# Block diagonal of local queries: placed by DMA, or copied there by GpSimd

## The chip, the cores and the metric

One core of one Trainium2 chip. The metric is the device time of one execution in microseconds, as the median over runs. The profile is of one further execution, with its own time.

## What is computed

```python
def _attn_ref(q, k, v):              # 8 batches, 8 heads, 576 positions, 64 wide
    scores = q @ k.T / sqrt(64)
    mask_local   = (rel >= 0) & (rel < 32)            # rel = row - column; heads 0 to 3
    mask_strided = (rel >= 0) & (same position modulo 32)   # heads 4 to 7
    attn = softmax(where(mask, scores, -1e9))
    return attn @ v

def _moe_ref(x, w_gate, w1, w2):     # x: 4608 tokens x 512; 8 experts, 1024 wide
    expert = argmax(x @ w_gate)                        # one expert a token
    gate = softmax(x @ w_gate)[expert]
    out = gate * (relu(x @ w1[expert]) @ w2[expert])
```

The attention's output, heads side by side, is the `x` of the second part. All is fp32.

## The kernel before, in words

The program has an attention stage (to about 220 us) and an expert stage. They overlap: the first experts' windows, over the tokens of the first four batches, are laid between the last batches' attention (`fillers`).

**Attention.** A batch is cut into five tasks (`BANK_PAIRS`), 40 in all. A task fills one PSUM bank of 128x512 scores. Tasks k=0 and k=1 are local, each for two heads: the 512 queries are 16 blocks of 32, and a block sees 64 keys. `wide` (L408 to L412) makes one matmul a block for both heads: the stationary operand is a block diagonal of 128x64, with head 0's 32 queries on partitions 0 to 63 and head 1's on partitions 64 to 127, and zeros elsewhere. Zeros are written once. Queries come from the host with the block as the last index, so that a block's 64 columns stand 16 floats apart:

```python
q = qkl[k][:, 0:2 * LQ].rearrange("p (q j) -> p q j", j=LB)     # L409, LB = 16
nc.tensor.matmul(sb[...], q[:, :, j], qkl[k][:, k0:k0 + 64], ...)   # L411
```

Tasks k=2 to 4 are strided heads and rests (`local` L419, `strided` L424). In every task a bf16 matmul first puts the mask into the bank (L403).

A task runs through three stages. `stage_s` makes the scores, then `softmax` (L349 to L363): maximum and subtraction on VectorE, exponential on ScalarE, sum and reciprocal on VectorE, product with the reciprocal on GpSimd (L362). `stage_t` (L453), three tasks later, transposes the probabilities on TensorE, and ScalarE moves them to SBUF. Four tasks later, values are multiplied (`av_local` L478, `av_strided` L467). A finished pair of batches is routed (`logits`, `route`), and `xrows` (L515 to L523) transposes tokens into rows: GpSimd writes the gate into 16 columns behind the row (L517), ScalarE copies the row (L521, shown as its helper's line L162), and ScalarE's queue sends it to memory (`xd`). Five row buffers rotate.

**Loads.** SP's queue issues queries and keys five tasks ahead (`load_qk`), values (`load_v`) and expert weights (`wload` L214, 1 MB each; `wsplit` L219 splits them into two parts on ScalarE, L222, and VectorE, L223). A local task takes three loads (L381 to L383): partitions 64 to 127 whole, and partitions 0 to 63 in two pieces, as head 0's queries lie in other columns than head 1's. Two buffers, `qkl`, serve k=0 and k=1.

**Order.** TensorE's order in the attention stage is the one that the program is written in. The other engines' queues are ordered by a scheduler, which plans with its own idea of durations; an engine then works strictly in that order. `issue_after` puts an instruction behind another on the same queue.

## Time and profile before

| | |
|---|---|
| median of three timed runs | 665.07 us (664.34 to 665.81) |
| profiled execution, its own time | 671.04 us |
| its span, first to last instruction | 668.8 us |
| TensorE matmul busy | 626.7 us, 94% |
| VectorE busy | 400.9 us, 60% |
| ScalarE busy | 327.3 us, 49% |
| GpSimd busy | 148.1 us, 22% |
| DMA moved | 149.85 MB, mean 224 GB/s |

In the rows, PE is TensorE's matmuls and PEld its weight loads, DVE is VectorE, ACT ScalarE, POOL GpSimd, and SP the engine whose queue issues loads. L12 is a line of the kernel. `out<-in` names what an instruction writes and reads. A matmul in fp32 shows as two records. `[1.60 <-X]` is idle time of the engine ahead of an instruction, and what ended it. Durations of matmuls that follow each other overlap; from start to start is what one costs. The granted clock is a share of TensorE's full 2.4 GHz.

### The profile page before, as it was taken

The numbers are of one execution on the slowest core, as the hardware profiler recorded it, in microseconds if no ns is written. First come the engines' busy times: TensorE is split into PE (matmuls) and PEld (weight loads), VectorE is DVE, ScalarE is ACT, GpSimd is POOL, SyncE is SP. The second block draws the span as 40 slices with busy tenths as digits, with TensorE's granted clock in tenths as the row PEclk, the third lists the DMA queues.
The fourth block names the chain that finished last, engine by engine and source line by source line (L and its number), as shares of the span: only waits on it lengthen the run. The fifth ranks groups of instructions, "written<-read, shape, count | busy, mean of one in ns | idle before, by whom it ended". The sixth has DMA issues, their size and how long they took to land.

```text
span 668.8 us, 14979 instructions
## 1 busy us (share of the span) xinstructions
PE 626.7 (94%) x6136; PEld 522.0 (78%) x6154; DVE 400.9 (60%) x788; ACT 327.3 (49%) x584; POOL 148.1 (22%) x168
## 2 busy tenths in 40 slices
PE   4999889789979999999899899999999999999996
PEld 3877778577858778888588788887898788887885
DVE  5667968656757369899424576823596235863332
ACT  1556665565645565356332555622565224753232
POOL 3232223420041021216100413200612004301021
PEclk9899999989989999899999999999999999999999
DMA  9968998994652865558933576872896546863301
GB/s 283 243 231 270 299 302 256 333 342 162 222 212 96 300 225 167 179 193 280 384 142 117 204 292 209 282 252 92 314 356 219 170 181 225 328 238 150 126 20 64
DMA packets 36550, 149.85 MB, mean 224 GB/s; under 512 B 5114, under 2 KB 5504, under 8 KB 26240
## 3 DMA queue, kind: packets, MB, share of 16 engines
q1 hardware_dynamic: 22848, 105.92, 47.1%
q10 hardware_dynamic: 7344, 22.70, 9.5%
q0 software_dynamic: 6288, 20.26, 8.3%
q8 instruction: 49, 0.80, 0.5%
q14 instruction: 21, 0.17, 0.1%
HBM read 129.69 MB, written 19.63 MB: 223 GB/s over the span
## 4 chain that ended last, share of the span: by engine, by line
PE 35%; issue 34%; POOL 7%; DMA 5%; DVE 4%; ACT 2%; POOLq 1%; ACTq 0%; another core or an unknown queue 0%
POOL xg L239 4%; PE t L297 4%; PE t L299 4%; PE t L298 4%; PE y L286 4%; PE y L287 3%; PE y L288 3%; POOL out_dram L258 2%; PE s L411 2%; DMA raw<-in_wcat_dram 1%; PE v L520 1%; DMA out_dram<-y,oids 1%; PE v L467 1%; DMA xg<-xd,eids 1%; DMA xd<-xr 1%
## 5 line engine op out<-in xcount | busy, mean ns | idle before, releaser
L223 DVE TENSOR_TENSOR wlo<-raw,whi 128x1024 fp32r<-128x1024 f32 x136 | 164.0, 1222 | 76.2 <-ACT whi L222 68.1
L222 ACT CAST whi<-raw 128x1024 fp32r<-128x1024 f32 x136 | 139.3, 1051 | 63.4 <-PE s L288 25.4
L297 PE MATMUL t<-xh,whi 128*128 128x256 f32 (+1 forms) x384 | 126.9, 332 | 2.3 <-ACT xh L231 2.1
L298 PE MATMUL t<-xl,whi 128*128 128x256 f32 (+1 forms) x384 | 124.3, 324 | 0.0
L299 PE MATMUL t<-xh,wlo 128*128 128x256 f32 (+1 forms) x384 | 123.6, 322 | 0.5 <-DVE wlo L223 0.5
L303 DVE SCALAR_TENSOR_TENSOR hl<-t,hh 128x256 fp32r<-128x256 f32 (+1 forms) x96 | 49.0, 510 | 103.2 <-ACT hh L302 102.9
L302 ACT ACTIVATE hh<-t 128x256 fp32r<-128x256 f32 (+1 forms) x96 | 43.8, 456 | 120.7 <-PE t L299 109.2
L297 PEld LDWEIGHTS t<-xh,whi 128*128 128x128 f32 x384 | 73.1, 191 | 13.3 <-ACT xh L231 3.3
L286 PE MATMUL y<-whi,hh 128*128 128x512 f32 x192 | 77.2, 402 | 2.1 <-ACT hh L302 2.1
L299 PEld LDWEIGHTS t<-xh,wlo 128*128 128x128 f32 x384 | 73.6, 192 | 6.3 <-DVE wlo L223 1.1
L298 PEld LDWEIGHTS t<-xl,whi 128*128 128x128 f32 x384 | 73.4, 191 | 5.9 <-DVE xl L232 0.3
L287 PE MATMUL y<-wlo,hh 128*128 128x512 f32 x192 | 75.9, 395 | 0.0
L288 PE MATMUL y<-whi,hl 128*128 128x512 f32 x192 | 74.6, 395 | 0.0
L362 POOL TENSOR_TENSOR prob<-prob,ri 128x512 f32<-128x512 f32 x40 | 42.5, 1063 | 122.9 <-DVE ri L361 87.6
L258 POOL DMA_INDIRECT out_dram<-y,oids x24 | 27.5, 1147 | 115.7 <-DVE y L257 110.9
L162 ACT COPY xT<-v 128x270 f32<-128x270 f32 (+1 forms) x80 | 30.1, 480 | 28.8 <-PE v L467 12.3
L286 PEld LDWEIGHTS y<-whi,hh 128*128 128x128 f32 x192 | 36.4, 189 | 9.4 <-ACT hh L302 2.9
L288 PEld LDWEIGHTS y<-whi,hl 128*128 128x128 f32 x192 | 35.9, 189 | 9.1 <-DVE hl L303 1.3
L287 PEld LDWEIGHTS y<-wlo,hh 128*128 128x128 f32 x192 | 36.5, 190 | 5.0
L358 DVE TENSOR_REDUCE sm<-prob 128x8 f32<-128x512 f32 x40 | 27.3, 683 | 21.5 <-ACT prob L356 21.2
L352 DVE TENSOR_REDUCE nm<-s 128x8 f32<-128x512 f32 x40 | 27.3, 683 | 18.5 <-PE s L411 14.0
L239 POOL DMA_INDIRECT xg<-xd,ids x24 | 30.2, 1259 | 31.9 <-ACT xh L231 18.9
(219 smaller groups left out, 1056.7 us busy)
## 6 DMA issues: line engine op xcount, KB each, us to landing
raw<-in_wcat_dram SPq DMA_DIRECT2D x68, 1024.0 KB
sraw<-in_wcat_dram ACTq DMA_DIRECT2D x12, 1024.0 KB
xd<-xr ACTq DMA_DIRECT2D x36, 264.0 KB
vl<-in_vv_dram SPq DMA_DIRECT2D x16, 512.0 KB
qkl<-in_qk_dram SPq DMA_DIRECT2D x16, 264.0 KB
vt<-in_vv_dram SPq DMA_DIRECT2D x16, 256.0 KB
qk<-in_qk_dram SPq DMA_DIRECT2D x8, 484.0 KB
qk<-in_qk_dram SPq DMA_DIRECT2D x8, 432.0 KB
```

Source lines behind the costliest of these rows:

```text
L222: nc.scalar.copy(out=hi[:, sl], in_=raw[:, sl])
L223: i = nc.vector.tensor_tensor(out=lo[:, sl], in0=raw[:, sl], in1=hi[:, sl].bitcast(F32), op=ALU.subtract)
L239: lastp[0] = nc.gpsimd.indirect_dma_start(out=xg, out_offset=None, in_=xd[0:rows, :], in_offset=bass.IndirectOffsetOnAxis(ap=idc, axis=0))
L286: nc.tensor.matmul(yb[t], hh[:, ts], whi[:, w], start=(j == 0), stop=False)
L287: nc.tensor.matmul(yb[t], hh[:, ts], wlo[:, w], start=False, stop=False)
L288: nc.tensor.matmul(yb[t], hl[:, ts], whi[:, w], start=False, stop=(j == 7))
L297: nc.tensor.matmul(hb[:, 0:n], whi[:, w], xh[:, dc, :], start=(dc == 0), stop=False)
L298: nc.tensor.matmul(hb[:, 0:n], whi[:, w], xl[:, dc, :], start=False, stop=False)
L299: nc.tensor.matmul(hb[:, 0:n], wlo[:, w], xh[:, dc, :], start=False, stop=(dc == 3))
L302: nc.scalar.activation(out=hh[:, 0:n], in_=hb[:, 0:n], func=AF.Relu)
L303: nc.vector.scalar_tensor_tensor(out=hl[:, 0:n], in0=hb[:, 0:n], scalar=0.0, in1=hh[:, 0:n].bitcast(F32), op0=ALU.max, op1=ALU.subtract)
L362: lastp[0] = nc.gpsimd.tensor_tensor(out=pv, in0=pv, in1=ri.unsqueeze(2).broadcast_to([128, 8, 64]), op=ALU.mult)
```

## The change

Queries and keys of a local task come in one load of all 128 partitions, queries in their natural order. A new tile `qbd` holds the block diagonal, block by block, 64 columns each; its zeros are written once. A new function, `spread`, copies the two heads' queries there on GpSimd, two tasks ahead of the task that reads them, and `issue_after` puts the copies behind the product of the task that was just begun. `wide` takes its weights from `qbd`, 64 floats side by side.

```diff
+AHEAD = 2
-        qkl = [loc.tile([128, 2 * LQ + LK], F32, name=f"qkl{k}") for k in range(2)]
+        qkl = [loc.tile([128, LQ + LK], F32, name=f"qkl{k}") for k in range(2)]
+        qbd = [loc.tile([128, LB, 2 * QB], F32, name=f"qbd{k}") for k in range(2)]
         for k in range(2):
-            nc.vector.memset(qkl[k][64:128, 0:LQ], 0.0)
-            nc.gpsimd.memset(qkl[k][0:64, LQ:2 * LQ], 0.0)
+            nc.vector.memset(qbd[k].rearrange("p j q -> p (j q)"), 0.0)
...
                 if k < 2:
-                    o = QKO[k]
-                    nc.sync.dma_start(out=qkl[k][64:128, LQ:], in_=qk[b, 64:128, o:o + LQ + LK])
-                    nc.sync.dma_start(out=qkl[k][0:64, 0:LQ], in_=qk[b, 0:64, o:o + LQ])
-                    nc.sync.dma_start(out=qkl[k][0:64, 2 * LQ:], in_=qk[b, 0:64, o + LQ:o + LQ + LK])
+                    nc.sync.dma_start(out=qkl[k], in_=qk[b, :, QKO[k]:QKO[k + 1]])
...
+        def spread(i):
+            if i < len(tasks) and tasks[i][1] < 2:
+                k = tasks[i][1]
+                for h in range(2):
+                    hs = slice(64 * h, 64 * h + 64)
+                    c = nc.gpsimd.tensor_copy(out=qbd[k][hs, :, QB * h:QB * h + QB],
+                                              in_=qkl[k][hs, 0:LQ].rearrange("p (j q) -> p j q", q=QB))
+                    if lastp[0] is not None:
+                        issue_after(c, lastp[0])
...
             def wide(j, i, col, last):
-                q = qkl[k][:, 0:2 * LQ].rearrange("p (q j) -> p q j", j=LB)
-                k0 = 2 * LQ + QB * j
-                nc.tensor.matmul(sb[64 * i:64 * i + 64, col:col + 64], q[:, :, j], qkl[k][:, k0:k0 + 64],
+                k0 = LQ + QB * j
+                nc.tensor.matmul(sb[64 * i:64 * i + 64, col:col + 64], qbd[k][:, j, :], qkl[k][:, k0:k0 + 64],
...
         def xrows(g, c, xT):
             xr = xrp.tile([128, XW], F32, name="xr")
-            nc.gpsimd.tensor_copy(out=xr[:, DM:XW], in_=gates[g][:, c:c + 1].broadcast_to([128, XW - DM]))
...
             evac(X_ENG[c % 2], xr[:, 0:DM], xb)
+            nc.scalar.copy(out=xr[:, DM:XW], in_=gates[g][:, c:c + 1].broadcast_to([128, XW - DM]))
...
         load_qk(0)
+        spread(0)
...
         load_qk(1)
+        spread(1)
...
                     pvs[i] = stage_s(*tasks[i])
+                    spread(i + AHEAD)
                     load_qk(i + NBK)
```

Smaller edits: the masks of three kinds of task become overlapping stretches of one tile, with 1,152 columns cast at the start instead of 1,536; the input tiles of tasks 2 to 4 get a buffer each of their exact width, where three equal buffers rotated; a table of 32 columns in `slot_tables` is made in a scratch buffer; the host no longer reorders the queries.

The scheduler also orders the queues anew. On GpSimd's queue, from the first softmax product on, gates stood between products (`xr` is a row buffer, `gt` the gates). Before:

```order
L362 TENSOR_TENSOR prob<-prob,ri 128x512 x9
L517 COPY xr<-gt 128x16 x3
L362 TENSOR_TENSOR prob<-prob,ri 128x512 x5
L517 COPY xr<-gt 128x16 x3
L362 TENSOR_TENSOR prob<-prob,ri 128x512
L517 COPY xr<-gt 128x16 x2
```

Now:

```order
L391 COPY qbd_137<-qkl_135 64x16x32 x2
L391 COPY qbd_138<-qkl_136 64x16x32 x2
L362 ISA
L362 TENSOR_TENSOR prob<-prob,ri 128x512 x4
L391 COPY qbd_137<-qkl_135 64x16x32 x2
L362 TENSOR_TENSOR prob<-prob,ri 128x512
L391 COPY qbd_138<-qkl_136 64x16x32 x2
L362 TENSOR_TENSOR prob<-prob,ri 128x512 x4
```

The gates are gone, and the copies for a local task stand right behind the product of the task two before it.

On SP's queue, at the turn from the second batch's loads to the third's (`vl` and `vt` are values, `raw` expert weights). Before:

```order
L387 DMA qk<-in_qk_dram 128x864
L394 DMA vt<-in_vv_dram 128x512
L381 DMA qkl_135<-in_qk_dram 64x1056
L382 DMA qkl_135<-in_qk_dram 64x512
L383 DMA qkl_135<-in_qk_dram 64x544
L394 DMA vl<-in_vv_dram 128x1024
L381 DMA qkl_136<-in_qk_dram 64x1056
```

Now:

```order
L401 DMA vt_360<-in_vv_dram 128x512
L384 DMA qk_358<-in_qk_dram 128x864
L215 DMA raw<-in_wcat_dram 128x2048
L380 DMA qkl_135<-in_qk_dram 128x1056
L401 DMA vl<-in_vv_dram 128x1024 x2
L380 DMA qkl_136<-in_qk_dram 128x1056
```

A first load of expert weights has moved ahead of the third batch's queries, and three more follow in the next 21 rows; before, the first stood some forty rows further on.

The splits of these weights on ScalarE and VectorE move with their loads: the first `whi` (L222, now L223) now stands between the two copies of the first batch's local values.

On VectorE's queue, at the first softmax (`nm` maximum, `sm` sum, `ri` reciprocal). Before:

```order
L352 TENSOR_REDUCE nm<-s 128x8
L355 TENSOR_TENSOR prob<-s,nm 128x512
L352 TENSOR_REDUCE nm<-s 128x8
L358 TENSOR_REDUCE sm<-prob 128x8
L355 TENSOR_TENSOR prob<-s,nm 128x512
L360 TENSOR_SCALAR ri<-sm 128x8
```

Now:

```order
L352 TENSOR_REDUCE nm<-s 128x8
L355 TENSOR_TENSOR prob<-s,nm 128x512
L352 TENSOR_REDUCE nm<-s 128x8
L355 TENSOR_TENSOR prob<-s,nm 128x512
L352 TENSOR_REDUCE nm<-s 128x8
L358 TENSOR_REDUCE sm<-prob 128x8 x2
L360 TENSOR_SCALAR ri<-sm 128x8
```

The first sum stood behind the second task's maximum; it now stands behind the third's.

## Rows read from the trace of the kernel before

**Rows 1.** Windows: length, busy us (instructions) PE, PEld, DVE, ACT, POOL; clock, DMA share, GB/s
```profile
42.00:61.50 19.50, 18.96 (x389) 14.20 (x389) 12.91 (x33) 11.23 (x26) 5.31 (x6) 1.00 0.83 259
61.50:83.00 21.50, 19.85 (x417) 16.70 (x419) 18.99 (x56) 14.09 (x30) 6.14 (x11) 1.00 0.87 275
...
104.00:125.00 21.00, 19.03 (x415) 16.09 (x414) 18.42 (x61) 13.92 (x30) 7.35 (x12) 1.00 0.90 283
125.00:145.00 20.00, 15.68 (x246) 13.18 (x252) 9.65 (x25) 9.30 (x19) 7.03 (x10) 0.91 0.99 318
...
300.00:668.00 368.00, 357.39 (x2243) 299.52 (x2241) 190.31 (x248) 165.49 (x265) 73.01 (x62) 0.99 0.59 211
```

**Rows 2.** Instructions of lines L411 and L478: duration ns min/median/max, first and last start
```profile
L411 PEld LDWEIGHTS s<-qkl x512: 184/206/228, 6.8 to 181.9; 128*64 128x64 f32 x171
...
L478 PEld LDWEIGHTS v<-pTl,vl x512: 132/138/158, 24.3 to 217.0; 128*64 128x64 f32 x171
```

**Rows 3.** Timeline of PE: start us, us, engine, line, operation
```profile
43.89 2.03 PE L478 MATMUL v<-pTl,vl 128*64 128x64 f32 x64
45.86 0.66 PE L520 MATMUL y<-cst,xT 128*128 128x128 f32 x4
...
47.09 2.06 PE L411 MATMUL s<-qkl 128*64 128x64 f32 x32
49.09 0.66 PE L453 MATMUL t<-cst,prob 128*128 128x128 f32 x4
```

**Rows 4.** Timeline of the start, all engines
```profile
6.85 2.12 PE L411 MATMUL s<-qkl 128*64 128x64 f32 x32 [1.60 <-DMA qkl<-in_qk_dram]
...
12.24 0.81 PE L424 MATMUL s<-qk 64*54 64x54 f32 x24
...
14.49 1.04 POOL L362 TENSOR_TENSOR prob<-prob,ri 128x512 f32<-128x512 f32 x1 [8.93 <-DVE ri L361]
...
15.58 1.12 PE L453 MATMUL t<-cst,prob 128*128 128x128 f32 x4 [2.54 <-POOL prob L362]
```

**Rows 5.** Windows of 2 us, columns as in rows 1
```profile
4.00:6.00 2.00, 0.58 (x1) 0.10 (x1) 1.36 (x6) 0.00 (x0) 1.25 (x2) 1.00 1.11 250
10.00:12.00 2.00, 2.00 (x37) 1.66 (x39) 0.75 (x2) 0.64 (x1) 0.00 (x0) 1.00 1.01 393
16.00:18.00 2.00, 2.00 (x27) 1.38 (x27) 0.12 (x1) 1.24 (x3) 1.04 (x1) 0.50 1.06 227
```

**Rows 6.** Instructions of single lines on POOL and DVE, columns as in rows 2
```profile
L371 POOL MEMSET qkl<- x2: 515/516/518, 0.8 to 1.2; 64x512 f32 x2
...
L362 POOL TENSOR_TENSOR prob<-prob,ri x40: 1037/1043/1823, 14.5 to 214.2; 128x512 f32<-128x512 f32 x40
...
L517 POOL COPY xr<-gt x36: 187/196/1184, 41.6 to 246.3; 128x16 f32<-128x16 f32 x36
...
L370 DVE MEMSET qkl<- x2: 485/485/485, 1.2 to 1.8; 64x512 f32 x2
```

**Rows 7.** Page, part 5: group xcount | busy us, mean ns of one | idle before, releaser
```profile
L358 DVE TENSOR_REDUCE sm<-prob 128x8 f32<-128x512 f32 x40 | 27.3, 683 | 21.5 <-ACT prob L356 21.2
L352 DVE TENSOR_REDUCE nm<-s 128x8 f32<-128x512 f32 x40 | 27.3, 683 | 18.5 <-PE s L411 14.0
```

**Rows 8.** Waits of POOL to 300 us: us in total, times, longest us
```profile
POOL prob L362 <- DVE ri L361: 87.6, 26, 9.7
...
POOL xr L517 <- DMA xd<-xr: 22.3, 3, 13.6
```

**Rows 9.** Timeline of SP's issues and of POOL: a load and a product
```profile
46.86 0.47 SPq L381 DMA_DIRECT2D qkl<-in_qk_dram  x1
...
58.49 1.04 POOL L362 TENSOR_TENSOR prob<-prob,ri 128x512 f32<-128x512 f32 x1 [1.48 <-DVE ri L361]
```

**Rows 10.** Chain of waits: start us, us, what (a DMA from issue to landing)
```profile
83.19 9.06 DMA raw<-in_wcat_dram
```

**Rows 11.** Timeline of ACT, a small copy
```profile
192.92 0.20 ACT L162 COPY xT<-v 128x64 f32<-128x64 f32 x1
```

More of the change, by code (lines that the diff above doesn't have):

```diff
@@ L183, in moe_attn @@
     wg_sb = const.tile([128, 4, 32], F32, name="wg_sb")
-    mask_b = const.tile([128, 3, 8, 64], BF16, name="mask_b")
+    mask_b = const.tile([128, 18, 64], BF16, name="mask_b")
     tri_b = const.tile([128, 128], BF16, name="tri_b")
@@ L320, in moe_attn @@
     with ExitStack() as actx:
-        inp = actx.enter_context(tc.tile_pool(name="inp", bufs=NBK - 2))
+        inp = actx.enter_context(tc.tile_pool(name="inp", bufs=1))
         loc = actx.enter_context(tc.tile_pool(name="loc", bufs=1))
@@ L334, in make_masks @@
         def make_masks():
-            for k, kinds in enumerate((((0, 1, 1), (1, 8, 0)), ((0, 2, 0), (2, 8, 2)), ((0, 8, 2),))):
-                for x0, x1, m in kinds:
-                    nc.vector.tensor_copy(out=mask_b[:, k, x0:x1, :],
-                                          in_=lmask_f[:, 64 * m:64 * m + 64].unsqueeze(1).broadcast_to([128, x1 - x0, 64]))
+            for x0, x1, m in ((0, 1, 1), (1, 10, 0), (10, 18, 2)):
+                nc.vector.tensor_copy(out=mask_b[:, x0:x1, :],
+                                      in_=lmask_f[:, 64 * m:64 * m + 64].unsqueeze(1).broadcast_to([128, x1 - x0, 64]))
         def load_more():
@@ L379, in load_qk @@
                 if k < 2:
-                    o = QKO[k]
-                    nc.sync.dma_start(out=qkl[k][64:128, LQ:], in_=qk[b, 64:128, o:o + LQ + LK])
-                    nc.sync.dma_start(out=qkl[k][0:64, 0:LQ], in_=qk[b, 0:64, o:o + LQ])
-                    nc.sync.dma_start(out=qkl[k][0:64, 2 * LQ:], in_=qk[b, 0:64, o + LQ:o + LQ + LK])
+                    nc.sync.dma_start(out=qkl[k], in_=qk[b, :, QKO[k]:QKO[k + 1]])
                     return
-                t = inp.tile([128, max(QKW[2:])], F32, name="qk")
+                t = inp.tile([128, QKW[k]], F32, name=f"qk{k}")
                 loaded[b, "qk", k] = t
                 nc.sync.dma_start(out=t[:, 0:QKW[k]], in_=qk[b, :, QKO[k]:QKO[k + 1]])
+        def spread(i):
[7 more added lines that the diff above has]
+                        issue_after(c, lastp[0])
         def load_v(i):
@@ L391, in load_v @@
                 b, k = tasks[i]
-                t = inv.tile([128, VVW[0]], F32, name="vl", bufs=2) if k < 2 else inv.tile([128, max(VVW[2:])], F32, name="vt", bufs=3)
+                t = inv.tile([128, VVW[0]], F32, name="vl", bufs=2) if k < 2 else inv.tile([128, VVW[k]], F32, name=f"vt{k}", bufs=1)
                 loaded[b, "v", k] = t
@@ L401, in stage_s @@
             sb = bank("s")
-            mk = 0 if k < 2 else k - 1 if k < 3 else 2
-            nc.tensor.matmul(sb, identb, mask_b[:, mk].rearrange("p n k -> p (n k)"), start=True, stop=False)
+            mk = 0 if k < 2 else 8 if k < 3 else 10
+            nc.tensor.matmul(sb, identb, mask_b[:, mk:mk + 8].rearrange("p n k -> p (n k)"), start=True, stop=False)
             t = loaded.get((b, "qk", k))
@@ L676, in slot_tables @@
             nc.vector.tensor_scalar(out=rem, in0=cnt, scalar1=-float(BASE), scalar2=0.0, op0=ALU.add, op1=ALU.max)
-            it128 = rt.tile([128, 32], F32, name="it128")
+            it128 = scratch(32)
             nc.vector.tensor_scalar(out=it128, in0=iota_sb[:, 0:32], scalar1=128.0, scalar2=None, op0=ALU.mult)
@@ L1163, in host_layout @@
                 parts = [lq[:, k, :, 0:LQ], lk[:, k, :, 0:LK]]
-                parts[0] = parts[0].reshape(B, 128, LB, QB).transpose(0, 1, 3, 2).reshape(B, 128, LQ)
             elif key[0] == "lx":
```

## The prediction, made before the changed kernel was run

> **What bounds the kernel now.** I first cut the span into stretches of about one batch each and read every engine's busy time there [rows 1]. TensorE is the fullest engine in every stretch: 18.96 of 19.50 us in the plain batch, and 357.39 of 368.00 us in the expert stage after 300 us, which the change hardly touches. So time can only be won before 300 us, by giving TensorE less to do or less to wait for. The same rows show how thin the cover is: VectorE has 18.99 of 21.50 us in a batch that also routes, the DMA engines move 259 to 318 GB/s at shares of 0.83 to 0.99, and from 125 to 145 us TensorE itself stands still for 4.3 us.
>
> Next I looked for TensorE work that is dear for its size. Two lines have the same shape: L411 (scores of local queries) and L478 (probabilities times values), both with a stationary operand of 128x64, 64 moving columns and two column halves of the array in turn. Their weight loads take 206 and 138 ns [rows 2]. Loads and matmuls overlap each other, so the pitch matters: 64 records of L478 pass from 43.89 to 45.86 us, 30.8 ns each; 32 records of L411 hold TensorE from 47.09 to 49.09 us, 62.5 ns each [rows 3]. (One fp32 matmul shows as two records: 16 matmuls a task make 32.) What differs is how the weights lie: in L411 the 64 queries stand 16 floats apart, in L478 side by side.
>
> **The change, part by part.** *Weights side by side.* If L411 falls to the pitch of L478, a task drops from 2.00 to 32 x 30.8 ns = 0.99 us. When L478 follows, its first loads already overlap the tail of L411, and the task costs nearer 1.9 us; I take 0.95 us saved. There are 16 tasks; the first two belong to the start, below. Of the other 14, ten stand where TensorE is full. Four do not: one ahead of each of the two routings, where VectorE has 18.99 of 21.50 and 18.42 of 21.00 us, and two in the 125 to 145 us stretch [rows 1]; I give those half. That is 10 x 0.95 + 4 x 0.48 = 11.4 us. The bounds are 6 us (half everywhere) and 14 x 1.02 = 14 us.
>
> Here a rule of the Trainium skill speaks against the change: the page "TensorE: Matmul & The Clock Gate", section "LDWEIGHTS (loading the stationary operand)", prices a weight load by its columns alone, which would make the loads of both lines equal and this term zero. The trace disagrees, with 206 against 138 ns for the same 64 columns [rows 2]. Another page of the skill, "SBUF — State Buffer", in its note on SBUF cachelines, says that reads more than 16 bytes apart lose bandwidth, which fits the 64 bytes here.
>
> *Start.* Before, the first task waits until 6.85 us for its load, the third ends at 13.05 us, the first softmax product starts at 14.49 and the first transpose at 15.58 us [rows 4]. The first load now comes as one transfer. While the loads of half the partitions ran, the DMA engines were full at 250 GB/s (4 to 6 us) and 227 GB/s (16 to 18 us), with transfers of all 128 partitions at 393 [rows 5]. At that rate the constants and the first load, 0.7 MB, need 1.8 us, so they land at about 4.2 us. GpSimd has then done its remaining memsets, of 0.52 us each [rows 6], and the two copies follow: first scores at 5.8, third task done near 9.9 us. VectorE's order now puts the maximum of the third task ahead of the first sum; from there it is 3.1 us of vector work (three reductions of 683 ns [rows 7], a subtraction about as long, the small reciprocal) and 1.04 us of product to the first transpose, at 14.1 us: 1.5 us won, the first two tasks included. VectorE's two memsets there now cover four times the elements of those that took 485 ns [rows 6], twice the columns, 1 us more in all ahead of the casts. Bounds: 3.5 won, 1 lost (dear copies, that microsecond; or TensorE, idle longer, staying longer at the granted clock of 0.50 that it has at 16 to 18 us, which is its 1.2 GHz level [rows 5]).
>
> *GpSimd's copies.* 32 copies of 64x512 are added, and the trace has none. A memset of that shape takes 515 ns, a two-input product of 128x512 takes 1043 [rows 6]; I take 0.6 us, near the memset, as a copy reads one operand. That is 19 us more on an engine that is busy 5 to 7 us in 20 [rows 1], and it hides: products wait 87.6 us in all for VectorE's reciprocals [rows 8], and a product is wanted only three tasks later. What the copies add is a wait for the load, with the next product behind them on the queue. In the tightest case before, the load was issued at 46.86 us, and the product that its copies would follow ends at 59.53 us: 12.7 us in hand [rows 9]. The slowest load on the chain of waits took 9.06 us from issue, for 1 MB [rows 10]. So I take 0, with 3 us lost as the bound.
>
> *Gates by ScalarE.* 36 copies of 128x16 leave GpSimd (196 ns each [rows 6]) and come to ScalarE, where a small copy also takes 0.20 us [rows 11]: 7.2 us over 36 places on an engine with 11.23 of 19.50 us [rows 1]. Its waits for rows still on their way to memory, 22.3 us in all, the longest 13.6 [rows 8], no longer stand ahead of products. ScalarE had to wait for the same buffers anyway. I take 0, with 2 us either way.
>
> *Queues.* Two of three query loads go, 32 issues on SP. Each batch's 1.08 MB of them takes about 2.7 us at 393 GB/s instead of 4.5 at 240. But the new order also pulls the first four weight loads of 1 MB into the first three batches. Before, the first was issued at 83.19 us, and its split could not start for another 9.06 us [rows 10]. I take it as even that the first batches now carry these loads and splits instead; I bound it by 4 us won and 3 lost (a split that now waits in the first batch). The second batch, at 259 GB/s in 19.5 us, becomes 17.5 us with the same 5.05 MB and some 1.4 MB of weights: 368 GB/s, just under the 393 that full transfers reached [rows 5]. I charge 1 us.
>
> *Nothing* for the packed masks (one of the five casts ahead of the first matmuls' needs was already covered by the load), exact tiles (same rotation) and the scratch tile (VectorE, a small operation).
>
> **The sum:** -11.4 - 1.5 + 0 + 0 + 0 + 1 = -11.9 us. The profiled execution took 671.04 us; it would take 659.1. It lies 5.97 us over the median of the three timed runs, 665.07, so the median should come to 653.2, say **653 us**.
>
> **The rivals.** *Another engine takes over* (0.12). With TensorE lighter, VectorE at 88% in routing batches or the DMA engines, at 368 of 393 GB/s by the estimate above, set the pace, and L411 gives half everywhere: -5.7 - 1.5 + 1, about 659 us. For it speak the shares in [rows 1], against it that TensorE's one plain wait for queries is the 1.60 us at the start [rows 4].
>
> *The spacing isn't the cause* (0.06). L411 also adds onto a bank already filled by the mask, which stays. Then only the start's single load and the DMA charge are left, near 665 us. The skill's rule on columns, above, would give the same. Against it speaks the longer weight load itself [rows 2].
>
> *Slower: GpSimd as the gate* (0.06). A copy stands for a late load with the next product behind it. From 12.7 us between issue and use it bites; a Pool wait as long as the 13.6 us of [rows 8] once a batch would use up the three tasks of slack and cost TensorE some 3 us, 21 over seven batches: 674 us. It turns the sign from 1.7 us a batch. For it speaks that four early weight loads share the queue; against it, 9.06 us as the worst landing and that each load gets shorter.
>
> **How the numbers follow.** My forecast has 0.76. Its terms run from -8 to about -20; with the first rival inside, 645 to 661 us leaves out the two rivals at 665 and 674 and a few per cent below. About 0.2% (1.3 us) is what these runs can tell apart: they spread over 1.47 us. Faster takes the forecast, the first rival and a little of the second: 0.90; same 0.04; slower 0.06.
>
> **What would show it.** Right: L411's weight loads near 138 ns and its 32 records in 1.0 us; TensorE's busy time before 220 us down by 12 to 15 us; products not waiting for copies; the expert stage as long as before. Wrong: weight loads still near 206 ns; TensorE idle more often in the second and third batch, with a weight split or a load as releaser; or GpSimd's copies held by a load, and transposes of probabilities released by products.

## Result: slower by 0.75%, and the profile after

The changed kernel takes 669.28 us in the median (667.30 to 671.52, 6 runs), the kernel before 664.71 us beside it (663.06 to 665.81, 6 runs): a ratio of 1.0075, with a 95% interval of 1.0047 to 1.0102. A second comparison, with later runs (e14 below), gave 1.0075 again (1.0048 to 1.0102). The prediction was 653 us, with 645 to 661 as its range. It had the sign wrong.

The two profiled executions hide this: the changed kernel's took 671.39 us, that of the kernel before 671.04, which lay 6 us over its own median. Where two traces are compared below, it is therefore mostly a second pair, e13 (before, 665.08 us) and e14 (changed, 666.97 us), both on one chip. That pair shows less than half of the loss: e14's traced execution lay 2.3 us under the median of its own run.

**What came as foretold.** One line's instructions, in the changed kernel (duration ns min/median/max, first and last start):

```profile
L417 PEld LDWEIGHTS s<-qkl,qbd x512: 132/138/232, 7.3 to 180.7; 128*64 128x64 f32 x171
...
  POOL qbd L391: 19.3, 15
```

and its timeline of TensorE, where the 32 records of L417 now stand 0.98 us ahead of the next line, against 2.00 in [rows 3]:

```profile
88.12 1.15 PE L417 MATMUL s<-qkl,qbd 128*64 128x64 f32 x32
89.10 2.04 PE L484 MATMUL v<-pTl,vl 128*64 128x64 f32 x64
```

The weight load fell from 206 ns [rows 2] to 138, exactly that of the line with its weights side by side. TensorE's busy time up to 220 us fell from 193.6 to 182.9 us, and from 196.0 to 186.2 in the pair e13 and e14: 10 to 11 us, not 12 to 15. So work did go, and more waiting came in its place. A copy on GpSimd takes 614 ns, as priced:

```profile
L391 POOL COPY qbd<-qkl x32: 601/614/790, 5.3 to 171.1; 64x512 f32<-64x512 f32 x32
```

**What did not.** The first of the two extracts above has the new wait in its last line: TensorE's two queues waited 19.3 us, 15 times, for the copies. They wait side by side: 11.7 us are the weight loads', 7.6 the matmuls'. All waits of TensorE's matmuls, the first three:

```profile
PE s L417 <- POOL qbd L391: 7.6, 6, 3.9
PE s L410 <- DVE mask_b L337: 6.8, 1, 6.8
PE t L459 <- POOL prob L362: 4.6, 3, 4.0
```

The longest one stands at the second batch's first local task. In the timeline of all engines there:

```profile
22.64 0.63 ACT L356 ACTIVATE prob<-prob 128x512 f32<-128x512 f32 x1
...
23.65 0.68 DVE L358 TENSOR_REDUCE sm<-prob 128x8 f32<-128x512 f32 x1
...
25.04 0.20 DVE L361 RECIPROCAL ri<-ri 128x8 f32<-128x8 f32 x1
25.38 1.04 POOL L362 TENSOR_TENSOR prob<-prob,ri 128x512 f32<-128x512 f32 x1 [5.72 <-DVE ri L361]
...
26.37 1.28 POOL L391 COPY qbd<-qkl 64x512 f32<-64x512 f32 x2
...
27.70 1.97 PE L417 MATMUL s<-qkl,qbd 128*64 128x64 f32 x32 [3.90 <-POOL qbd L391]
...
29.46 3.42 PE L484 MATMUL v<-pTl,vl 128*64 128x64 f32 x64
```

Read it from the bottom. The scores of task 5 (L417, 27.70) wait for two copies, which stand on GpSimd's queue behind the product of task 3 (25.38), which stands behind that task's reciprocal, sum and exponential. So the copies tie the scores of a local task to the whole softmax of the task two before it. And the wait is paid twice: the 32 records then take 1.97 us instead of 1.15, and L484 3.42 instead of 2.04. The windows of 2 us there (columns as in [rows 1]) show the granted clock at 0.50, its 1.2 GHz level, behind a stretch in which TensorE did nothing:

```profile
24.00:26.00 2.00, 0.00 (x0) 0.00 (x0) 1.59 (x5) 0.83 (x2) 0.62 (x1) 0.92 0.91 261
26.00:28.00 2.00, 0.30 (x6) 0.30 (x8) 1.09 (x3) 0.00 (x0) 1.86 (x4) 0.50 1.04 435
28.00:30.00 2.00, 2.00 (x44) 2.00 (x41) 0.28 (x1) 0.00 (x0) 1.93 (x3) 0.50 0.15 53
```

The windows by batch, as in [rows 1], show the price and what else is new:

```profile
42.00:61.50 19.50, 16.65 (x384) 12.63 (x384) 15.10 (x35) 14.35 (x33) 7.54 (x9) 1.00 0.94 319
61.50:83.00 21.50, 19.09 (x424) 15.45 (x425) 19.34 (x60) 13.21 (x34) 8.39 (x10) 1.00 0.96 343
...
125.00:145.00 20.00, 13.82 (x210) 11.55 (x212) 9.29 (x26) 8.30 (x20) 10.18 (x12) 0.83 0.71 241
```

TensorE has 2.3 us less to do in the first of them, and the DMA engines carry 319 and 343 GB/s instead of 259 and 275: the first expert weights come here now. Two of the four issues on SP's queue (the first was at 83.19 us before, [rows 10]):

```profile
23.41 0.42 SPq L215 DMA_DIRECT2D raw<-in_wcat_dram  x1
...
41.96 0.42 SPq L215 DMA_DIRECT2D raw<-in_wcat_dram  x1
```

**A ledger.** Each task begins with the weight load of its mask matmul, which makes 40 marks in a trace. At these marks e14 stands against e13 like this (us, plus is late; the mark of task 6 comes right behind the scores of task 5): task 0 +2.4, task 5 0.0, task 6 +4.7, task 21 +1.9, task 25 -0.3, task 36 -2.7, task 38 +0.4, task 39 +0.4. Scatters of results, from 317 us to the end, all stand at +2.2. So e14 loses 4.7 us to one wait and the half clock behind it, wins 7.4 in the next thirty tasks, loses 3.1 between tasks 36 and 38, and 1.8 more ahead of 317 us.

### The profile page after: what moved, and what is told of

Its sections match the earlier page's. It is cut to its first block, busy times and chain, and to the rows that moved or that the text cites. A ratio compares the mean times of both kernels' runs of the same rounds, so it can differ in the third digit from the quotient of the medians.

```text
span 669.6 us, 14978 instructions
## 1 busy us (share of the span) xinstructions
PE 616.8 (92%) x6136; PEld 513.1 (77%) x6154; DVE 405.2 (61%) x786; ACT 330.5 (49%) x620; POOL 159.5 (24%) x162
## 4 chain that ended last, share of the span: by engine, by line
PE 38%; issue 35%; DVE 10%; POOL 8%; ACT 4%; DMA 4%; POOLq 1%; ACTq 0%; another core or an unknown queue 0%; DVEq 0%
POOL xg L240 4%; PE t L298 4%; PE t L300 4%; PE t L299 4%; PE y L287 3%; PE y L288 3%; PE y L289 3%; POOL out_dram L259 3%; PE s L417 2%; DVE wlo L224 2%; PE v L484 2%; PE t L459 1%; PE s L430 1%; DVE prob L355 1%; DMA out_dram<-y,oids 1%
## 5 line engine op out<-in xcount | busy, mean ns | idle before, releaser
L223 ACT CAST whi<-raw 128x1024 fp32r<-128x1024 f32 x136 | 139.1, 1050 | 67.4 <-PE s L289 25.5
L298 PEld LDWEIGHTS t<-xh,whi 128*128 128x128 f32 x384 | 73.6, 192 | 12.7 <-ACT xh L232 3.6
L356 ACT ACTIVATE prob<-prob 128x512 f32<-128x512 f32 x40 | 25.2, 631 | 30.7 <-DVE prob L355 23.6
L352 DVE TENSOR_REDUCE nm<-s 128x8 f32<-128x512 f32 x40 | 27.3, 682 | 14.1 <-PE s L417 8.4
```

Of the source, the lines that this page charges most:

```text
L223: nc.scalar.copy(out=hi[:, sl], in_=raw[:, sl])
L298: nc.tensor.matmul(hb[:, 0:n], whi[:, w], xh[:, dc, :], start=(dc == 0), stop=False)
```

## Experiments

The first theory, from the trace after: the copies, behind a product, cost it. Its rivals: the early weight loads and splits, the later constants, the gates on ScalarE. After four runs a further one joined them (theory C): what L417 saves only becomes waiting, and waiting lowers TensorE's clock.

The table has ratios to the kernel before on the same chip. A ratio is not the quotient of the two medians that the text gives, and can lie up to 0.24% from it. "Late" is against e13's marks, in us. Marks of two traces of the kernel before (the first, and e13) differ by 1.1 at most up to task 36, and by 2.7 at task 39; those of the changed kernel (the first, and e14) by up to 2.7 ahead of task 36. Each trace is one execution; the last column says how far that lay over the median of its run. So differences under 3 us in these columns mean little. Chips differ too: the kernel before takes 664.5 us on one and 671.7 on another. In the traces of the slower chips 1.7 to 5.5 us of that lie between 363 and 499 us, behind all marks.

| run | what differs | ratio (95%) | late at task 6 | 21 | 36 | 39 | traced execution over median |
|---|---|---|---|---|---|---|---|
| e14 | the change | 1.0075 (1.0048 to 1.0102) | +4.7 | +1.9 | -2.7 | +0.4 | -2.3 |
| e1 | copies 3 tasks ahead | 1.0020 (0.9988 to 1.0053) | -0.6 | +3.2 | -2.4 | +2.7 | -0.2 |
| e2 | copies of the first 2 tasks only | 1.0018 (0.9986 to 1.0049) | -0.1 | +0.7 | -5.4 | -0.1 | -2.2 |
| e3 | constants first | 1.0045 (1.0016 to 1.0074) | +4.8 | +1.7 | -4.7 | +0.2 | -1.9 |
| e5 | weights held | 1.0057 (1.0028 to 1.0086) | +6.1 | +3.8 | 0.0 | +4.5 | +1.4 |
| e6 | 3 ahead, weights held | 0.9965 (0.9932 to 0.9997) | +0.5 | -3.5 | -7.8 | -3.1 | -0.8 |
| e7 | e6 and four more mask matmuls a local task | 0.9995 (0.9969 to 1.0021) | +2.1 | +2.1 | -2.0 | -2.2 | -1.1 |
| e11 | e6, gates on GpSimd | 0.9952 (0.9921 to 0.9984) | +1.9 | -0.6 | -3.7 | -3.8 | +4.0 |
| e12 | e6, constants first | 1.0039 (1.0004 to 1.0073) | +0.9 | -2.6 | -6.7 | -2.4 | -1.0 |
| e16 | e2, weights held | 1.0000 (0.9969 to 1.0030) | +1.5 | -1.4 | -5.8 | -1.5 | -0.7 |
| e18 | e16, gates on GpSimd | 0.9982 (0.9952 to 1.0012) | -0.5 | -3.8 | -6.6 | -6.7 | -2.6 |
| e13 | before itself | 1.0004 (0.9978 to 1.0030) | 0 | 0 | 0 | 0 | 0.0 |
| e15 | before, early weights | 1.0061 (1.0034 to 1.0088) | -0.5 | +6.1 | +2.4 | +2.4 | -2.4 |
| e17 | before, gates on ScalarE | 1.0015 (0.9986 to 1.0044) | +0.2 | -0.3 | +3.1 | +6.9 | +4.2 |
| e9 | before, four more mask matmuls | 1.0160 (1.0116 to 1.0204) | +1.9 | +5.2 | +8.1 | +7.7 | -4.8 |
| e4 | before, columns 4 floats apart | 1.0068 (1.0038 to 1.0098) | +0.4 | +1.1 | +2.6 | +6.9 | 0.0 |
| e8 | before, columns side by side by DMA | 1.0047 (1.0016 to 1.0078) | -2.0 | -5.4 | +1.4 | +5.4 | +1.1 |
| e10 | e8, weights at their old places | 0.9965 (0.9930 to 0.9999) | -0.3 | -5.2 | -7.7 | -7.9 | -2.7 |

Versions with held weights have lines shifted by 6 or 7.

### e1, e2, e3: the copies' place, the copies at all, the start

```diff
-AHEAD = 2
+AHEAD = 3
```

> The change with the copies three tasks ahead instead of two, behind the product of the task three before; nothing else differs. Theory (a copy stands behind a softmax product, so the scores of a local task are tied to the whole softmax of the task two before it): TensorE's waits for qbd, 19.3 us in all in the changed kernel, fall below 5 us, the idle stretch at 24 to 28 us and the granted clock of 0.50 behind it go, and the time falls from 669.3 to 660 to 664 us. Rival 1 (the early weight loads and splits cost it): unchanged, 668 to 670. Rival 2 (the later constants at the start cost it): unchanged, 668 to 670, with the waits for qbd gone. Rival 3 (gates on ScalarE): unchanged.

Measured: 672.99 us beside 671.72, a ratio of 1.0020. The waits for the copies were gone, as the theory had it:

```profile
PE s L417 <- POOL qbd L391: 0.3, 1, 0.3
```

The idle stretch at 24 us went with them (task 6 at -0.6 instead of +4.7). Against the change's 1.0075 that is 0.55%, some 3.7 us. But the time did not fall under that of before: by task 21 this version was 3.2 us late again. The wait is one loss of several.

```diff
                     pvs[i] = stage_s(*tasks[i])
-                    spread(i + AHEAD)
                     load_qk(i + NBK)
```

> The change with the copies of the first two tasks alone: all later local tasks compute with the first batch's queries (that part of the attention is left out), 28 copies less. It bounds what the copies, their place and their waits cost together, against what the weights side by side bring. Theory: 655 to 661 us, that is the gain of the narrower pitch less the loss at the start. Rivals 1, 2 and 3: 667 to 670 us, since weight loads, constants and gates stand as in the changed kernel.

Measured: 672.26 us, 1.0018, the same as e1. With 28 of 32 copies away, no more is won than by giving them a task more. So the copies' own time (17 us of GpSimd) costs nothing that these runs can tell; their place costs.

```diff
-        nc.scalar.dma_start(out=cst0, in_=blob0)
+        nc.sync.dma_start(out=cst0, in_=blob0)
```

> The change with the constants' load on SP's queue ahead of the first queries, instead of on ScalarE's queue. Theory: the constants land at 3.5 to 4 us again instead of 5.3, the first mask product starts near 4.7 to 5 us instead of 6.8; worth 1 to 2 us, 667 to 668.5 us, with the waits for qbd as they are. Rival 2 (the start is the whole loss): 664 us or less. Rivals 1 and 3: 669.

Measured: 674.32 us, 1.0045, somewhat under the change's 1.0075, with intervals that overlap. The constants landed earlier (task 0 at 0.0 instead of +2.4), and by task 5 both stood alike: the start carries through to nothing. Rival 2, that the start is the whole loss, is out. On top of e6 it was even slower than without (e12), of which more below.

### e4, e8, e10: another way to get the columns side by side

The kernel before, with queries interleaved by four instead of sixteen (e4), or not at all (e8), so that DMA writes pieces of 512 or 128 bytes. IL is 4 or 1:

```diff
-                q = qkl[k][:, 0:2 * LQ].rearrange("p (q j) -> p q j", j=LB)
+                q = qview(k)[:, j // IL, :].rearrange("p (q j) -> p q j", j=IL)
...
+                    for h in range(2):
+                        hs = slice(64 * h, 64 * h + 64)
+                        nc.sync.dma_start(out=qview(k)[hs, :, QB * IL * h:QB * IL * h + QB * IL],
+                                          in_=qk[b, hs, o:o + LQ].rearrange("p (g x) -> p g x", x=QB * IL))
+                    nc.sync.dma_start(out=qkl[k][:, 2 * LQ:], in_=qk[b, :, o + LQ:o + LQ + LK])
```

> The kernel before with one part changed: no copies, still written by DMA, but blocks interleaved by four instead of sixteen, so that a block's 64 columns stand 4 floats (16 bytes) apart; the two query loads write pieces of 512 bytes, the keys come in one load of 128 partitions. Gates stay on GpSimd, weights load late. If 16 bytes of spacing already give the narrow pitch (32 records in 1.0 us) and the copies and their order were what ate the gain: 653 to 658 us. If the pitch needs neighbours, or the gain is lost further down whatever the copies do: 663 to 666. If pieces of 512 bytes are dear to the DMA engines: above 666.

> The kernel before, but DMA writes the block diagonal with a block's 64 columns side by side, in pieces of 128 bytes; no copies, gates on GpSimd, and by the scheduler's order no weights before the last batches' queries. If the pitch needs neighbours, 32 records take 1.0 us here (at 16 bytes apart they did not), and TensorE's busy time falls by 12 us. If the pieces are cheap for the DMA engines: 0.98 to 0.99 of before; if they are dear: queries land late, TensorE waits for qkl, above 1.01.

The weight loads of the scores, e4 first (L418 in both):

```profile
L418 PEld LDWEIGHTS s<-qkl x512: 192/217/221, 7.1 to 185.4; 128*64 128x64 f32 x171
```

and e8:

```profile
L418 PEld LDWEIGHTS s<-qkl x512: 132/138/232, 7.0 to 183.2; 128*64 128x64 f32 x171
```

Four floats apart is as dear as sixteen; side by side is cheap. So e4 tells nothing of the pitch's worth. Against its expectation, its scheduler order had the weights early (first at 60.40 us, 83.19 before), and without any copies it was 0.68% slower than before. e8 had them late instead, and at task 31 it was 9.8 us ahead of e13. Then came this place:

```profile
132.94 11.43 SPq L215 DMA_DIRECT2D raw<-in_wcat_dram  x3
...
141.67 0.58 PE L298 MATMUL t<-xh,whi 128*128 128x256 f32 x1 [8.79 <-ACT whi L223]
```

Pieces of 128 bytes were thus no burden here; what made it 1.0047 was that three weight loads were issued when their expert was already due. e10 puts them where the kernel before has them:

> DMA writes the block diagonal side by side in pieces of 128 bytes (no copies, gates on GpSimd), now with the weight loads at the places that they have in the kernel before, instead of later. The run without that was 9.2 us ahead of before at 128 us and then stood 8.8 us for a weight split. If that was all that was lost: 0.985 to 0.992 of before, the fastest so far. If the lead is lost later in any case (waits and half clock): 0.997 to 1.003.

Measured: 661.55 us beside 663.68, 0.9965. In the trace the lead stays (-7.9 at task 39, 6.1 at the end), but that execution lay 2.7 us under its own median, and only about 2.1 us reach the median. The ratio lies between the two expectations, next to the second (0.997 to 1.003), which its interval covers; the first (0.985 to 0.992) is missed.

### e5, e6, e15: the early weights

```diff
+HOLD = (24, 34, 36, 37, 38, 39)
...
-        nc.sync.dma_start(out=raw, in_=wcat[...])
+        d = nc.sync.dma_start(out=raw, in_=wcat[...])
+        if nraw[0] < len(HOLD):
+            issue_after(d, qis[min(HOLD[nraw[0]], len(qis) - 1)])
+        nraw[0] += 1
```

`qis` holds the issues of `load_qk`. In the kernel before, the weights stand behind exactly these.

> The change with one part undone: the first six loads of expert weights are held on SP's queue to the places that they had before (behind the queries of tasks 24, 34, 36 to 39), so that no weights and no splits fall into the first four batches. Copies stay two tasks ahead. Theory A (copies behind the softmax cost most, early weights the rest): waits for qbd as in the changed kernel (near 19 us with the weight loads, 7.6 us of matmuls), time 0.2 to 0.5% under the changed kernel, 1.003 to 1.005 of before. Theory B (the early weights cost it): the value loads are no longer late, 0.99 to 1.00 of before. Theory C (the narrower pitch only turns TensorE's work into waits and half clock): 1.003 to 1.008, the total at granted clock 0.50 near 40 us as in the changed kernel.

> Copies three tasks ahead and the first weight loads held to their old places. Theory A and B: 0.985 to 0.993 of before (the forecast gain of some 11 us, less the start). Theory C: 0.998 to 1.004, with more us at granted clock 0.50 than the 20 of before.

Measured: with copies two ahead 672.76 us beside 669.72, 1.0057; with copies three ahead 668.04, 0.9965. Held weights alone gain 0.2%, which two intervals of 0.3% don't tell from nothing; together with copies three ahead they gain 0.55% on e1. The place of the copies is worth 0.9% here (e5 to e6). Theory B alone is out, and so is theory A alone; only both edits together bring the time under that of before. The forecast of 11 us did not come in either. Theory C fits e5's ratio; e6's lies between its range and that of the other two, with a mean granted clock of 0.976 over its runs against 0.983 in before beside them.

The early weights by themselves, in the kernel before:

```diff
+HOLD = (9, 13, 17, 19, 38, 39)
...
+        with tc.high_priority() if nraw[0] < 4 else ExitStack():
+            d = nc.sync.dma_start(out=raw, in_=wcat[...])
```

> The kernel before with one thing of the changed one: the first four loads of expert weights stand on SP's queue where the changed kernel has them (behind the queries of tasks 9, 13, 17 and 19), and the splits follow. If early weights and splits cost by themselves: 1.003 to 1.007 of before, with values or ScalarE's copies late between 30 and 85 us. If they cost only where TensorE runs ahead: 0.998 to 1.002.

Measured: 668.70 us beside 664.53, 1.0061. One thing of the changed kernel, four loads moved forward with their splits, costs by itself nearly as much as the whole change. Its timeline, SP's and TensorE's rows:

```profile
20.88 0.42 SPq L218 DMA_DIRECT2D raw<-in_wcat_dram  x1
...
36.54 0.99 PE L474 MATMUL v<-pT,vt 54*64 54x54 f32 x33 [3.26 <-issue]
```

and the landings of 24 to 44 us (KB each, median us from issue to landing), in e15:

```profile
vl<-in_vv_dram SPq DMA_DIRECT2D x2, 512.0 KB, 9.4
...
qkl<-in_qk_dram SPq DMA_DIRECT2D x2, 264.0 KB, 8.5
```

against e13:

```profile
vl<-in_vv_dram SPq DMA_DIRECT2D x2, 512.0 KB, 5.3
...
qkl<-in_qk_dram SPq DMA_DIRECT2D x2, 264.0 KB, 4.1
```

The values and queries of local tasks (`vl`, `qkl`) come some 4 us later there; those of the other tasks (`vt`, `qk`) 1 us or less. TensorE waited once for such a load, 1.5 us at 92 us. Its longest wait, the 3.26 us at 36.54, makes most of the 3.8 us lost between tasks 6 and 10, and for it the profile names no releaser (`issue`). It stands in the middle of one task's values, with 14 records done and 33 to go; e13 has no such wait there. That the weight load caused it is argued, not shown. At task 21 this version is 6.1 us late, and part of that comes back when the weights are wanted (+2.4 from task 36 on).

### e7, e9: is TensorE the bound?

Four more mask matmuls in each local task, which leave the scores' mask a mask: 0.9 us a task, about 14 us in 16 tasks. In the kernel before (e9) and in e6 (e7):

```diff
-            nc.tensor.matmul(sb, identb, mask_b[...], start=True, stop=False)
+            for r in range(5 if k < 2 else 1):
+                nc.tensor.matmul(sb, identb, mask_b[...], start=(r == 0), stop=False)
```

> The kernel before with four more bf16 mask matmuls of 128x512 in each local task (0.9 us a task, 14 us in all) and the weight loads held to the places that they have there anyway. It asks whether TensorE's work is the bound in the kernel before, as the prediction took it to be. If it is: 10 to 14 us slower, 1.015 to 1.02 of before. If TensorE's full windows already hold slack: under 4 us slower, 1.00 to 1.005.

> As the run with copies three tasks ahead and weights held, but each local task puts its mask into the bank five times instead of once (four more bf16 matmuls of 128x512, about 0.9 us a task, 14 us in all), so that TensorE has as much work as before again. If TensorE's work bounds the attention stage, it is 10 to 14 us slower than that run. Theory C (what L417 saves turns into waiting and half clock): within 3 us of it.

Measured: e9 675.72 us beside 663.68, 1.0160, that is 10.6 us more. e7 668.72 us, against 668.04 of e6, 0.3% by the ratios, within the 3 us that theory C gave. The kernel before was bound by TensorE, as the prediction said. With L417's microsecond gone, the same work can be put back nearly for nothing. How that goes is seen in the window of 170 to 195 us, e6:

```profile
170.00:195.00 25.00, 19.79 (x223) 16.36 (x223) 15.09 (x36) 12.46 (x28) 8.43 (x7) 0.80 0.60 213
```

and e7:

```profile
170.00:195.00 25.00, 22.12 (x337) 18.47 (x334) 18.91 (x41) 15.68 (x35) 7.60 (x7) 1.00 0.75 252
```

At task 36 the extra matmuls have cost 5.8 us (-2.0 instead of -7.8); then e6 falls to half clock, with 4.7 us lost up to task 39, and e7 does not. The median of the mean granted clock over the runs is 0.976 in e6 and 0.989 in e7 (0.983 in before beside them).

### e13, e14: before and change on one chip

> The kernel before itself, for a profile on the same chip as the next three runs: 1.000 within 0.3%, at granted clock 0.50 for about 20 us, near 669 us less what the profiled execution of it was over its median (6 us).

> The changed kernel itself, again: 1.005 to 1.010 of before, at granted clock 0.50 for some 40 us; second batch 5 us late against before by the sixth task, level with it near 120 us, and then no lead.

Measured: 665.03 and 669.26 us. The traces give the ledger above. The place where 3.1 us go, between tasks 37 and 38, in TensorE's timeline of e13:

```profile
191.74 0.66 PE L520 MATMUL v<-cst,xT 128*128 128x128 f32 x4 [1.32 <-ACT xT L162]
```

and of e14:

```profile
181.25 0.44 PE L276 MATMUL v<-cst,xg 128*128 128x128 f32 x2 [1.03 <-ACT xr L163]
183.22 0.67 PE L525 MATMUL v<-cst,xT 128*128 128x128 f32 x4 [1.10 <-DVE xl L233]
188.05 1.00 PE L473 MATMUL v<-pT,vt 54*64 54x54 f32 x52 [0.52 <-DVE xl L233]
190.66 1.12 PE L525 MATMUL v<-cst,xT 128*128 128x128 f32 x4 [1.60 <-ACT xT L163]
```

Four transposes take 1.12 us there and 0.66 in e13: TensorE is at half clock, which the windows of 4 us confirm, e14's being

```profile
184.00:188.00 4.00, 3.28 (x49) 2.05 (x47) 4.00 (x9) 1.26 (x4) 1.42 (x2) 0.61 0.69 193
188.00:192.00 4.00, 2.35 (x59) 2.24 (x59) 2.35 (x5) 1.91 (x6) 0.55 (x1) 0.82 0.83 275
192.00:196.00 4.00, 3.94 (x26) 3.70 (x26) 0.42 (x1) 2.15 (x6) 0.50 (x1) 0.75 0.37 141
```

with 1.00 in all of e13's. The last loss stands in the expert stage. ScalarE's 96 writes of hidden values (`hh`) can be set against each other one by one: e14 is at -0.4 us at 295 us and at +2.2 from 314 us on. VectorE makes tables for the second half's tokens there, in four sets. The first and the last of them in e13:

```profile
275.41 0.56 DVE L746 TENSOR_TENSOR prob<-cst,skey 128x387 f32<-128x387 f32 x1
...
286.88 0.60 DVE L751 TENSOR_SCALAR prob<-prob,cst 128x387 bf16<-128x387 f32 x1
```

and in e14:

```profile
282.82 0.55 DVE L752 TENSOR_TENSOR prob<-cst,skey 128x387 f32<-128x387 f32 x1
...
300.82 0.61 DVE L757 TENSOR_SCALAR prob<-prob,cst 128x387 bf16<-128x387 f32 x1
```

They end 14 us later, and the last of them now stand among other tables (`am`) and weight splits (`wlo`) that TensorE waits for, in e14:

```profile
296.74 0.53 PE L761 MATMUL v<-prob,am 128*128 128x86 bf16 x9 [0.69 <-DVE am L748]
300.49 0.38 PE L300 MATMUL t<-xh,wlo 128*128 128x256 f32 x1 [0.82 <-DVE wlo L224]
```

From 296 to 302 us VectorE is busy all the time and TensorE for 4.49 of 6.00 us; in e13 TensorE is busy for all 6.00:

```profile
296.00:302.00 6.00, 4.49 (x38) 3.85 (x38) 6.00 (x10) 1.25 (x2) 0.11 (x1) 1.00 0.73 221
```

Every trace of a version built on the changed kernel loses 2.6 to 7.6 us between these two marks (e14 2.6, e6 6.2, e11 4.7, e18 5.6). Those built on the kernel before lose nothing there (-0.4 to 0.0), but for e17 (1.5), whose tables come late too. Up to 363 us some of it comes back: 0.0 to 5.1 us are left in the first group, -2.5 to +0.7 in the second. So this is a part of the change's loss that no run undoes; which of the change's edits moved the tables was not tested.

### e11, e16, e17, e18, e12: the gates, free copies, and one that stays open

Gates back on GpSimd in e6 (e11, whose edit is shown), and the reverse in the kernel before, gates alone moved to ScalarE (e17):

```diff
             xr = xrp.tile([128, XW], F32, name="xr")
+            nc.gpsimd.tensor_copy(out=xr[:, DM:XW], in_=gates[g][...])
...
-            nc.scalar.copy(out=xr[:, DM:XW], in_=gates[g][...])
```

> Copies three tasks ahead, weights held, and the gates back on GpSimd ahead of the rows' transposes, as before the change. If gates on ScalarE cost something: under 0.9965 of before, by up to 2 us. If they help, as products no longer stand behind rows on their way to memory: up to 3 us over it. Neither: within 0.2% of 0.9965.

> The kernel before with the gates copied by ScalarE behind the rows instead of by GpSimd ahead of them, the weight loads kept at their places; nothing else. In all traces so far with gates on ScalarE and no extra matmuls, TensorE ran at granted clock 0.50 for 7 to 14 us between 178 and 195 us; of eight with gates on GpSimd, three did. If the gates on ScalarE bring that: 1.003 to 1.006 of before, task 38 late by 3 us or more against the profile of before on its own chip. If it comes from TensorE running ahead: 0.998 to 1.002, full clock there.

Measured: e11 662.11 us beside 663.68, 0.9952; e17 666.02 beside 664.49, 1.0015. Neither is to be told from its neighbour (0.9965 and 1). e11 has the lowest ratio of all, and beats both kernels, the one before by 0.2 to 0.8% (0.24% by the medians). e17's trace is late by 3.8 us between tasks 36 and 39, as its first expectation has it, but that execution lay 4.2 us over its median; the ratio meets the second.

Copies for two tasks alone, weights held, gates on ScalarE (e16) or GpSimd (e18); e18 is e2's edit, e5's and e11's together:

> The change with copies for the first two tasks alone (all later local tasks compute with the first batch's queries, so that part of the attention is left out) and the weight loads held: nothing is left of the copies' time and waits, nor of early weights. It shows what the side-by-side weights are worth if the copies were free. By the forecast: 0.982 to 0.985 of before. By theory C (the lead goes into waits and half clock from the fifth batch on): 0.993 to 0.997, the same as with copies three tasks ahead.

> Copies for the first two tasks alone (later local tasks compute with the first batch's queries, so that part of the attention is left out), weights held, gates on GpSimd: all that is left of the change is the weights side by side and the one load of queries. The same with gates on ScalarE gave 1.000. If gates on ScalarE cost through the clock at 180 to 195 us: 0.992 to 0.996, full clock there. If the lead is lost there in any case: 0.998 to 1.002.

Measured: e16 664.56 us beside 664.53, 1.0000; e18 662.76 beside 664.49, 0.9982. In e18's one trace TensorE keeps full clock at 180 to 195 us, and the lead of 6.6 us at task 36 is still there at task 39; in e16's it shrinks from 5.8 to 1.5. Half clock between 175 and 215 us is seen in ten of the eleven traces with gates on ScalarE (not in e7), and in three of the nine with gates on GpSimd (the first of before, e4, e8). So it goes with the gates, but comes without them too. In time, gates on ScalarE are dearer in all three pairs, by 0.13% (e6 to e11), 0.15% (e17) and 0.18% (e16 to e18), each within the noise. Over all its runs e18's mean granted clock was 0.980, e16's 0.977, that of before 0.985: its one full trace is better than its runs. The gates are not shown to be the cause. Free copies don't bring the forecast either.

> Copies three tasks ahead, weights held, and the constants' load first on SP's queue. The start of the run with copies three ahead and weights held stood 1.8 us behind before at the first task, and 0.5 at the sixth; if that carries through: 0.994 to 0.996 of before. If it is lost in waits further on: 0.996 to 1.000.

Measured: 666.34 us beside 663.68, 1.0039, slower than e6 by 0.7%, though its marks stand as early up to task 36 (-6.7). Earlier constants change the scheduler's plan; what of it costs here stays open.

## Why the prediction was wrong, step by step

Four steps failed, and a small one besides (the start). The term for the weights was right in its cause and several times too large. The copies were said to hide, and did not. The queues were called even, and were not. And the expert stage, "which the change hardly touches", lost time.

**Weights side by side (-11.4).** The mechanism was right, to the number: 138 ns, and at full clock 0.98 to 1.08 us a task for the 0.99 foretold. The rule that a weight load costs by its columns (the Trainium skill, "TensorE: Matmul & The Clock Gate", "LDWEIGHTS (loading the stationary operand)") does not hold for these loads: 138, 206 and 217 ns for the same 64 columns. Wrong was the next sentence, "ten stand where TensorE is full", each taken with the whole 0.95 us. Full means that more work costs (e9: 10.6 us for 14), not that less work gains as much. With copies and early weights out of the way the lead at task 36 is 3.7 us in e11 and 5.8 to 7.8 in the others (e6, e10, e12, e16, e18), half of 14 x 0.95 or so, and by their ratios these runs end between 3.2 us under the kernel before (e11) and 2.6 over it (e12). The pitch is most by itself in e10, which has no copies: 2.3 us by its ratio, with 0.1 to 4.6 as the interval. The first rival had this mechanism (another engine takes over). Its price was half everywhere, about the lead at task 36; what is left at the end is less. The traces show two losses behind that task: TensorE falls to half clock (e6 against e7), and the expert stage's tables come late.

**GpSimd's copies (0, bound 3 lost).** This step named the wrong cover. It said that the copies hide since "a product is wanted only three tasks later". But a copy stands behind a product, and is itself wanted two tasks later. Behind the product of task j-2 stand its exponential, sum and reciprocal, and behind those two engines' queues; the scores of task j inherit all of it. The step looked for a load that comes late (12.7 us in hand, [rows 9]); apart from 0.9 us at the start, no query load did. (One copy, at 136.5 us, stood 4.5 us behind a gather of tokens, where TensorE waited for such gathers itself.) Measured by e1 and e6: 0.55 to 0.9%, that is 3.7 to 6 us. The slower rival had the place, GpSimd as the gate, and the wrong releaser.

**Queues (even, 4 won to 3 lost; +1 for DMA).** e15 prices the early weights alone at 0.61%, 4.1 us, beyond the bound. The estimate compared mean rates with the best rate (368 against 393 GB/s) and found room. A load's landing time is not a mean: values and queries of local tasks took 8.5 to 9.4 us instead of 4.1 to 5.3 with weight loads among them. How that became 4.1 us is only in part seen: 1.5 us of waiting for a load, and 3.26 us with no releaser named.

**Start (-1.5).** The copies came no later than the constants; those landed behind the query loads. From the timeline of the first changed trace:

```profile
5.27 1.27 POOL L391 COPY qbd<-qkl 64x512 f32<-64x512 f32 x2 [0.85 <-DMA qkl<-in_qk_dram]
5.31 0.64 DVE L855 CAST identb<-cst 128x128 bf16<-128x128 f32 x1 [2.10 <-DMA cst<-in_blob_dram]
...
6.77 0.58 PE L410 MATMUL s<-mask_b,identb 128*128 128x512 bf16 x1 [6.77 <-DVE mask_b L337]
...
17.26 1.11 PE L459 MATMUL t<-cst,prob 128*128 128x128 f32 x4 [3.97 <-POOL prob L362]
```

The first transpose came at 17.26 us, not at 14.1, and not at 15.58 as before [rows 4]. And the two tasks there gained little by the pitch. They took 1.98 us each, the first of them

```profile
7.28 1.98 PE L417 MATMUL s<-qkl,qbd 128*64 128x64 f32 x32
```

against 2.12 [rows 4] and 2.19 us. (In e14 the second took 1.15.) That is as long as the same records take at granted clock 0.50 (see the last section), though the clock column reads 1.00 at 6 to 12 us in both kernels; why is not shown. The estimate had taken the narrow pitch there. By task 5 all was level again; the term is nought.

**Gates (0, 2 either way).** Within the bound: ScalarE was dearer by 0.13 to 0.18% in three pairs, about 1 us, none to be told from nothing.

**The expert stage, and the small edits ("nothing").** The prediction left all time after 300 us as it was. In e14 2.6 us go between 295 and 314 us, where TensorE waits for VectorE, whose tables stand 7 to 14 us later than in e13. The change has VectorE's queue ordered anew; which of its edits moved the tables is open. One of those put at nothing, the scratch tile, stands in the same function as these tables.

The sum from what was measured: 0 to 3 us won by the pitch where copies and weights no longer cost (1.0000 to 0.9952: e16, e18, e6, e10, e11; the late tables are in all of these but e10, and e12 won nothing), 3.7 to 6 lost by the copies' place, up to 4 by the early weights. That can be up to twice the 4.6 us lost. The parts need not add: a TensorE that is late for one reason may wait less for the next.

## What to carry to other kernels

An instruction put behind another on a queue inherits all that the other waits for: count back from what it releases to the first engine that can be late, not only to its own data. Where a fullest engine is at 97%, price less work for it at what the next engine allows, and test it the other way round, with work added. And look where the scheduler puts the work of a later stage, its large transfers and its tables: that may cost more than the edit.

## What the runs showed of the hardware

- Weights four floats apart (16 bytes) load as slowly as those sixteen apart, 217 and 206 ns, and neighbours in 138. The Trainium skill, "SBUF — State Buffer", in its note on cachelines, gives four fp32 as the stride that is still free; the measurement (e4) differs.
- At granted clock 0.50 the side-by-side weights bring next to nothing. 32 records in e13 (columns 16 floats apart) and in e14 (side by side), in windows of 2 us that read 0.50:

```profile
138.10 2.10 PE L411 MATMUL s<-qkl 128*64 128x64 f32 x32
```

```profile
136.13 1.98 PE L417 MATMUL s<-qkl,qbd 128*64 128x64 f32 x32
```

- DMA pieces of 128 bytes did no harm that shows: e8 moved 37,882 packets under 512 bytes where e13 moved 5,114, and e10, with the same loads, is a little faster than the kernel before.
- A wait of a few us can cost TensorE more than the wait: behind the 3.90 us that end at 27.70 us it worked on at granted clock 0.50 until 32.5 us. The Trainium skill, "TensorE: Matmul & The Clock Gate", "HAM oscillation — how this bites in real kernels", describes the like for waits for DMA in a loop; here the wait was for copies. In e7 added matmuls were nearly free, with full clock where e6 had half.
